# Normalised linear attention feeding a gated-convolution FFN on one core: the first head pair's three loads as fp32 on two hardware queues, three casts on two engines, and a new order

## The chip, the cores and the metric

The kernel runs on one core of one Trainium2 chip. A core has five engines with an instruction stream each: TensorE (matmul, written PE in the profile, its weight loads PEld), VectorE (DVE), ScalarE (ACT), GpSimd (POOL) and SyncE (SP), and 16 DMA engines which all of them feed. The metric is the device time of one execution in microseconds (us); lower is better. The kernel before takes 180.41 us, the median of three runs (180.30 to 180.98).

## The reference

For each of 8 batches and 8 heads (576 rows, head size 64) a 64x64 product of k and v is formed over the rows and applied to q. The rows of the result are normalised by their root mean square over the head, scaled by `g_norm`, and the heads are put side by side as rows of 512. A feed-forward part follows: a product with `w_in` (512 to 1024) and a ReLU, a three-tap convolution along the rows, a sigmoid of it as a gate, and a product with `w_out` (1024 to 512).

```python
kv = np.einsum('bhsd,bhse->bhde', k, v)
out = np.einsum('bhsd,bhde->bhse', q, kv)
rms = np.sqrt(np.mean(out * out, axis=-1, keepdims=True) + 1e-06)
x = (out / rms * g_norm).transpose(0, 2, 1, 3).reshape(B, S, H * D)
h = np.maximum(x @ w_in, 0.0)
hp = pad(h, 1)                                  # one zero row on either side
conv_out = sum(conv_w[k] * hp[:, k:k + S, :] for k in range(3))
gate = 1.0 / (1.0 + np.exp(-conv_out))
return (h * gate) @ w_out
```

Inputs and output are fp32; the kernel computes its products in bf16.

## The kernel before

The program is one list of tokens, `ORDER`, run from front to back. Each token is the name of a small operation with its arguments, such as `hm.0.3` for batch 0 and column block 3. Behind `@` stand the slots (PSUM banks, or places in a ring of SBUF buffers) that it takes, and behind `:` a choice of engine. At the end of the kernel a chain of dependences holds every engine to the order in which its instructions were emitted. So an engine never passes an instruction that waits, and the order decides who waits for whom. What `:1` means depends on the operation. For `kvc`, `kvn`, `ky`, `oc`, `re` and `ea` a plain token runs on ScalarE and `:1` on VectorE; for `qc0` and `qc` it is the other way round (helper `copy`, L337).

The work on batch 0 goes by head pairs t = 0 to 3, two heads in one 128-partition tile:

- `qt0.0.t` transposes q on TensorE (L378, 12 matmuls) and `qc0.0.t` copies it out of PSUM (L339 on ScalarE).
- `kv.0.t.1` forms the product of k and v (L356, 12 matmuls). `kvc.0.t.1.0` and `kvc.0.t.1.1` copy its two 64x64 blocks into the block-diagonal `kvbd`.
- `ot.0.t` applies it to q (L428 and L429, 64 and 512 columns). `sq` squares the result on ScalarE, `on` sums the squares over a head by a matmul with `ones`, `nl` takes the reciprocal root on ScalarE, and `mu0` multiplies on VectorE into the tile xT. For the last pair `sqh`, `onh`, `nlh` and `muh` do the same in halves.

Batch 1 takes two pairs at a time (`qt`, `qc`, `kv.1.t.2`), later batches four (`kv.b.0.4`, 48 matmuls). From batch 2 on the norm goes another way: `ss` gathers the sums of squares, `ln` takes the root, `sl` splits it into two bf16 parts, `sp` spreads it over the heads by matmuls (L601), and `mu` multiplies on VectorE.

The feed-forward part works by batch b and block f of 128 columns. `hm.b.f` is the product with `w_in` (L619, 8 matmuls), `re.b.f` the ReLU (L625 on ScalarE, L627 on VectorE). For a convolution group c of one or two batches, `ta`, `aa` and `ab` form the three taps on VectorE, `sg` the sigmoid on ScalarE (L680) and `mg` the gated product on VectorE (L686). `om.p.m.f0` is the product with `w_out` for 128 output rows (L696). `om` takes all eight blocks at once for p = 1 and 2; for p = 0 and 3 it takes four, so `om.3.m.0` needs the first four blocks and `om.3.m.4` the rest. `ea` copies it out and `st` stores it from SyncE. `oh`, `eh` and `sh` do the very last row block in two halves of 256 columns.

`unread.n` issues n matmuls on a constant tile, `fill`, into a bank that nobody reads (L425). They keep TensorE occupied where the order has nothing else for it.

The loads: `pre` (L215 to L239) issues those of batch 0. The first pair's k and v come as fp32 from SyncE's queue into a staging tile `stg`, and `ca` (L326) casts them to bf16 on VectorE. All other loads of q, k and v go out from GpSimd's queue, which casts to bf16 on the way: the first pair's q, then q, k and v of pairs 1 to 3. Between them GpSimd finishes the identity matrix (L236). `Lq`, `Lk` and `Lv` load the other batches, `Li` a quarter of `w_in` and `Lo` a half of `w_out`, all from GpSimd's queue. Two small rows, `g_norm` and the convolution weights, go out from ScalarE's queue (L221, L224) ahead of ScalarE's first table load (L211). `ct` transposes them on TensorE (L251), `pg` copies them out and `pc` prepares the weights. `pi`, `ps` and `pn` make small constants on VectorE.

Of the kernel before, what the change touches and what calls it, by code (L numbers as in the profile page):

```python
# [51 lines left out]
FP32 = mybir.dt.float32  # L52
# [11 lines left out]


ORDER = """
pre@0,0,0 pi unread.10@0 qt0.0.0@0 qc0.0.0:1@0 ps pn ca.k.0 ca.v.0 kv.0.0.1@1 kvc.0.0.1.0:1@0 kvc.0.0.1.1 Lq.1.0@1
ct@2 qt0.0.1@3 pg ot.0.0@0 pc unread.3@4 kv.0.1.1@2 Lk.1.0@1 qc0.0.1:1 kvc.0.1.1.0:1 Lv.1.0@1 sq.0.0@0 kvc.0.1.1.1:1
on.0.0@4 ot.0.1@2 qt0.0.2@6 nl.0.0@0 sq.0.1@1 unread.4@7 kv.0.2.1@7 on.0.1@4 qc0.0.2:1@1 al.x0@0 mu0.0.0 kvc.0.2.1.0
kvc.0.2.1.1:1 qt0.0.3@6 nl.0.1@1 ot.0.2@0 Li.0 unread.3@7 kv.0.3.1@7,4 mu0.0.1 sq.0.2@2 qc0.0.3:1 al.h0@0  # L70
kvc.0.3.1.0 on.0.2@2 kvc.0.3.1.1:1 ot.0.3@6 nl.0.2@2 sqh.0.3.0@3 Li.3 mu0.0.2 unread.3@5 onh.0.3.0@2 sqh.0.3.1
nlh.0.3.0@3 onh.0.3.1 Lq.1.2 nlh.0.3.1 qt.1.0@0 qc.1.0:1@2 Lv.1.2 unread.7@5 kv.1.0.2@0 muh.0.3.0 muh.0.3.1
kvc.1.0.2.0@1 kvc.1.0.2.1 unread.2@5 ot.1.1@0 sq.1.1@4 hm.0.0@6 on.1.1@2 hm.0.1@4 re.0.0 nl.1.1@4 ta.0.0@0 mu0.1.1
ot.1.0@6 hm.0.6@2 hm.0.7@0 Lk.1.2 re.0.1 sq.1.0@5 re.0.6 ta.0.1 aa.0.0 ta.0.6@1 on.1.0@2 qt.1.1@4 re.0.7 kv.1.2.2@0
nl.1.0@5 ab.0.0 qc.1.1@3 kvc.1.2.2.0 Li.1 kvc.1.2.2.1 ta.0.7 mu0.1.0 Lv.2.0@0 unread.3@1 ot.1.2@0 Li.2 Lk.2.0@0
ot.1.3@4 sq.1.2@6 unread.2@2 on.1.2@6 Lq.2.0@0 Lk.3.0@1 aa.0.3 sq.1.3@7 on.1.3@2 ab.0.3 nl.1.2@6 hm.0.3@6 nl.1.3@7
mu0.1.2 sg.0.0 hm.0.2@0 sg.0.1 re.0.2 mu0.1.3 hm.1.2@4 hm.0.5@2 sg.0.7 sg.0.6 re.0.3:1 Lv.3.0@1 pl mg.0.0 hm.1.3@6
hm.1.0@0 ta.0.2@0 al.x1@1 re.0.5 re.1.2 ta.0.3 re.1.0 mg.0.3 kv.2.0.4@2 aa.0.1 re.1.3 al.h1@1 ab.0.1 hm.1.1@4
ta.1.2@1 ta.1.3 hm.0.4@6 hm.1.7@0 aa.1.1 kvc.2.0.4.0@0 sg.0.2 sg.0.3 kvc.2.0.4.1 re.1.1 re.0.4 re.1.7 Lq.3.0@1
qt.2.0@2 qt.2.1@4 mg.0.1 hm.1.5@6 ab.1.1 ta.0.4@0 qc.2.0@4 Lo.0 sg.1.2 sg.1.3 ot.2.0@2 ta.0.5 hm.1.4@0 re.1.5  # L80
sq.2.0@0 qc.2.1@0 oc.2.0@0 mg.1.1 ot.2.2@4 ot.2.1@6 re.1.4:1 sq.2.2@1 kv.3.0.4@2 aa.0.2 oc.2.2@1 ot.2.3@0
kvc.3.0.4.0:1@1 sq.2.1@2 ab.0.2 ta.1.0@1 oc.2.1 sq.2.3@3 hm.1.6@4 ss.2@3 qt.3.1@6 re.1.6:1 sg.0.5 qt.3.0@4 oc.2.3
kvc.3.0.4.1:1 sg.0.4 qc.3.1@1 qc.3.0@2 ta.1.1 ln.8@0 unread.1@0 ot.3.3@6 unread.1@0 ot.3.0@4 Lo.1 ot.3.2@0 sq.3.0@4
mg.0.2 oc.3.0@2 Lq.4.0@0 aa.1.0 om.0.0.0@2 ta.1.4@0 sl.8@0 ta.1.5 ab.1.0 aa.1.2 sq.3.2@5 om.0.1.0@3 oc.3.2@3
om.0.2.0@4 sq.3.3@6 ot.3.1@0 om.0.0.4 oc.3.3 om.0.2.4 sq.3.1@7 oc.3.1 sp.2.0@6,0 ea.0.0@0 ss.3@5 ea.0.2@1 om.0.3.0@2
mu.2.0.0 ln.1@0 mu.2.0.1 sp.2.1@4,6 Lv.4.0@0 om.0.3.4 Lk.4.0@0 mu.2.1.0 qtp.4.0@0 sg.1.0 mu.2.1.1 sl.1@0 hm.2.6@4
qc.4.0:1@3 hm.2.2@6 re.2.6 ea.0.3@2 ab.1.2 re.2.2 sp.3.0@4,0 sg.1.4 sg.1.1 om.0.1.4 mu.3.0.1 mu.3.0.0 kv.4.0.4@2
sg.1.5 kvn.4.0.4 sp.3.1@0,6 ky.4.0.4.0 ea.0.1@3 hm.2.5@4 ky.4.0.4.1 re.2.5 mu.3.1.1 mu.3.1.0 hm.2.4@6 Lq.5.0@1
Lk.5.0@1 Lv.5.0@1 re.2.4 hm.3.4@0 mg.1.0 mg.1.2 oq.4.0@4 oq.4.1@2 re.3.4 hm.3.5@6 Lv.6.0@0 sq.4.0@0 ta.1.6@1
hm.3.7@0 oc.4.0@0 hm.3.3@4 re.3.5 sq.4.1@1 oc.4.1 re.3.7 Lk.6.0@0 ta.1.7 ta.2.4@0 qtp.4.1@6 aa.1.3 hm.2.3@2 ta.2.5  # L90
ab.1.3 om.0.7.0@0 re.3.3 qc.4.1@4 sg.1.7 sg.1.6 oq.4.2@6 oq.4.3@4 aa.2.2 mg.1.3 ab.2.2 re.2.3 kv.5.0.4@1 kvn.5.0.4:1
sq.4.2@2 oc.4.2@1 sq.4.3@3 hm.3.6@2 oc.4.3 re.3.6 sg.2.5 ky.5.0.4.0:1 qtp.5.1@6 al.x2@0 Lk.7.0@1 Lv.7.0@1 om.0.7.4
qc.5.1@0 ta.2.6@1 sg.2.4 qtp.5.0@2 ky.5.0.4.1:1 qc.5.0@1 hm.2.7@6 hm.3.2@4 re.2.7 oq.5.2@2 ea.0.7@4 oq.5.3@6
sq.5.2@4 re.3.2 Lq.6.0@0 oc.5.2@3 Lq.7.0@1 mg.2.2 om.0.6.0@1 om.0.4.0@0 ta.2.7 oq.5.0@4 oq.5.1@2 sq.5.3@5 oc.5.3
ta.2.2@0 om.0.4.4 sq.5.0@6 ss.4@6 sq.5.1@7 kv.6.0.4@7 ta.2.3 aa.2.3 ss.5 oc.5.0@2 hm.3.1@4 om.0.6.4 oc.5.1 aa.2.1
ln.2@0 ab.2.3 hm.3.0@2 re.3.1 kvn.6.0.4 ea.0.4@5 re.3.0 ea.0.6@6 sl.2@0 hm.2.1@4 ab.2.1 hm.2.0@6 sp.4.0@0,2 re.2.1
om.0.5.0@4 mu.4.0.0 mu.4.0.1 re.2.0 sp.5.1@6,0 mu.5.1.1 kv.7.0.4@5 om.0.5.4 st.0.1 st.0.0 dq.6.0@2 sp.5.0@0,2 st.0.7
kvn.7.0.4:1 kx.7.0.4.0 kx.6.0.4.0 sg.2.7 sg.2.3 kx.6.0.4.1 sg.2.2 sg.2.6 mu.5.1.0 mu.5.0.0 om.0.8.0@5 mu.5.0.1
sp.4.1@6,0 mu.4.1.0 mu.4.1.1 om.0.8.4 al.h2@0 dq.6.1@3 ea.0.8@7 st.0.3 hm.5.2@2 re.5.2 ea.0.5@3 dq.7.0@4 hm.4.2@6
st.0.2 mg.2.1 hm.5.0@0 mg.2.3 oq.6.0@4 re.4.2 ta.2.0@0 oq.6.1@2 re.5.0 sq.6.0@0 hm.5.7@6 oc.6.0@2 sq.6.1@1 dq.7.1@0  # L100
hm.5.3@0 hm.4.3@4 re.5.7 oc.6.1 oq.6.2@6 re.5.3 sq.6.2@2 re.4.3 oc.6.2@3 hm.4.5@2 ta.2.1 st.0.8 aa.2.0 hm.4.1@0
hm.5.5@4 hm.5.1@6 ta.3.2@1 ab.2.0 ta.3.3 re.4.5 sg.2.1 re.4.1 hm.4.0@2 sg.2.0 st.0.5 kx.7.0.4.1 re.5.1 re.5.5 re.4.0
aa.3.1 ab.3.1 hm.5.4@0 mg.2.0 hm.4.6@6 hm.4.4@4 re.5.4 om.1.5.0@0 ta.3.0@0 oq.7.0@2 re.4.6 sg.3.3 oq.6.3@6 sg.3.2
sq.7.0@3 ea.1.5@0 ta.3.1 sq.6.3@4 re.4.4 om.1.4.0@1 oc.6.3 oc.7.0@0 ea.1.4@4 al.x3@1 om.1.7.0@0 oq.7.2@2 oq.7.1@6
oq.7.3@4 aa.3.0 ea.1.7@2 ss.6@1 sq.7.1@5 sq.7.2@6 mg.3.1 om.1.6.0@0 sq.7.3@7 ab.3.0 oc.7.1 ss.7 ln.3@0 oc.7.2@1
om.1.3.0@6 ea.1.6@1 om.1.1.0@7 ta.3.4@1 ta.3.5 aa.3.2 oc.7.3 ab.3.2 sl.3@0 sp.7.0@4,0 mu.7.0.0 om.1.0.0@2 mu.7.0.1
sp.6.0@0,4 om.1.2.0@3 ea.1.3@7 sg.3.0 sg.3.1 ea.1.0@3 mu.6.0.0 mu.6.0.1 hm.5.6@4 mg.3.0 st.1.7 st.1.4 st.0.6 st.0.4
ea.1.2@2 sp.6.1@2,0 om.1.8.0@6 mu.6.1.1 sg.3.5 re.5.6 ea.1.1@4 mu.6.1.0 ea.1.8@6 ta.3.6@0 sp.7.1@2,4 hm.4.7@0
al.h3@1 re.4.7 mu.7.1.1 mu.7.1.0 hm.6.1@6 sg.3.4 hm.7.0@0 hm.6.0@2 hm.7.1@4 ta.3.7 re.6.1 hm.7.6@6 aa.3.3 mg.3.2
re.7.0 re.6.0 ab.3.3 re.7.1 re.7.6 hm.7.5@4 hm.6.2@6 hm.7.2@2 hm.7.3@0 sg.3.6 sg.3.7 re.6.2 re.7.5 hm.7.7@6 re.7.3  # L110
re.7.2 ta.4.0@1 re.7.7 ta.4.1 hm.6.3@4 hm.6.5@2 re.6.3 hm.6.4@4 hm.7.4@6 aa.4.0 mg.3.3 st.1.3 ab.4.0 ta.4.2@0 sg.4.0
sg.4.1 ta.4.3 re.6.4 aa.4.1 re.7.4 re.6.5 mg.4.0 ab.4.1 hm.6.6@0 hm.6.7@4 re.6.6 re.6.7 om.2.4.0@2 sg.4.3 om.2.2.0@3
om.2.1.0@4 om.2.7.0@5 om.2.6.0@0 om.2.3.0@1 sg.4.2 ta.4.4@1 ta.4.5 aa.4.2 ea.2.4@5 st.1.8 st.1.6 st.1.0 om.2.8.0@2
st.1.5 st.1.1 mg.4.1 ab.4.2 ea.2.2@7 ta.4.6@0 ta.4.7 aa.4.3 ea.2.1@6 sg.4.4 ea.2.7@1 sg.4.5 st.2.1 ab.4.3 ea.2.6@3
ea.2.3@0 mg.4.2 sg.4.7 sg.4.6 om.2.5.0@3 om.2.0.0@1 mg.4.3 om.3.1.0@0 ea.2.8@4 ea.2.5@6 st.2.2 st.2.8 om.3.3.0@3
oh.3.8.0@4 om.3.3.4 om.3.1.4 om.3.2.0@2 om.3.5.0@6 om.3.2.4 st.1.2 st.2.3 ea.2.0@7 eh.3.8.0@4 om.3.5.4 st.2.0
ea.3.3@2 st.2.4 om.3.0.0@3 ea.3.1@0 om.3.6.0@7 om.3.0.4 ea.3.2@7 ea.3.5@5 st.3.3 om.3.6.4 om.3.4.0@6 st.2.7
om.3.7.0@2 ea.3.0@2 om.3.4.4 st.3.2 om.3.7.4 ea.3.6@1 ea.3.4@7 st.3.5 st.3.1 st.2.5 st.3.0 st.2.6 st.3.6 sh.3.8.0
ea.3.7@5 st.3.4 st.3.7 oh.3.8.1 eh.3.8.1 sh.3.8.1
"""  # L120


# [1 line left out]
def kernel(  # L124
# [11 lines left out]
    nc = tc.nc  # L136
    B, H, S, D = q.shape
# [3 lines left out]
    R = 6  # L141
# [32 lines left out]
    def heads(x, b, h0, n):  # L174
        return src[x][b, h0:h0 + n].rearrange("h (p r) d -> p h (r d)", r=R)
# [39 lines left out]
    def pre():  # L215
        for x in "qkv":
            qkv[x, 0] = ring(x, [PS, H, R * D], BF16, name=x + "_sb")
        T["stg"] = work.tile([PS, 2, 2, R * D], FP32, name="stg", tag="h0", bufs=1)
        for i, x in enumerate("kv"):
            nc.sync.dma_start(out=T["stg"][:, i], in_=heads(x, 0, 0, 2))  # L220
        nc.scalar.dma_start(  # L221
            out=cw_rows[NC:].rearrange("p (i d) -> p i d", i=2),
            in_=g_norm.unsqueeze(0).unsqueeze(0).to_broadcast([1, 2, D]))
# [7 lines left out]
        for i in range(2):  # L231
            nc.vector.memset(ones[i * D:(i + 1) * D, i * D:(i + 1) * D], 1.0)
        nc.vector.memset(kvbd[1], 0.0)
        for n, (x, t) in enumerate([(x, t) for t in range(NT) for x in "qkv" if t or x == "q"]):
            if n == 2:
                nc.gpsimd.affine_select(  # L236
                    out=ident, in_=ident, compare_op=AL.not_equal, fill=1.0,
                    base=0, pattern=[[-1, P]], channel_multiplier=1)
            nc.gpsimd.dma_start(out=qkv[x, 0][:, 2 * t:2 * t + 2, :], in_=heads(x, 0, 2 * t, 2))  # L239
# [83 lines left out]

    @op
    def ca(x, t):
        nc.vector.tensor_copy(qkv[x, 0][:, 2 * t:2 * t + 2, :], T["stg"][:, "kv".index(x)])  # L326

    def last():
        return nc.cur_bb.bb.instructions[-1]
# [7 lines left out]
    def copy(to, fr, on_act):  # L337
        if on_act:
            nc.scalar.activation(to, fr, AX.Copy)  # L339
        else:  # L340
            nc.vector.tensor_copy(to, fr)
# [439 lines left out]
```

## Time and profile before

| | us |
|---|---|
| median of three runs | 180.41 |
| the profiled execution | 180.37 |
| its span, first to last instruction | 178.6 |
| idle TensorE from 20 to 40 us / from 40 to 60 us | 1.08 / 0.48 |
| first real matmul (L378) | 5.85 |
| first matmul of the feed-forward part (L619) | 19.61 |
| last matmul ends | 174.46 |

The page's second part shows the span in 40 equal slices of some 4.5 us; a digit is the busy share in tenths.

```profile
PE   6999997999999999999999999999999999999990
DVE  5544199799999899999999999968999999930000
ACT  2479679999999999999999999999789986853341
POOL 7985528005320210600000000000000000000000
DMA  5999999999999999999939700420340003046574
```

TensorE is occupied nearly everywhere, with the caution that a busy matmul row also holds fills. VectorE and ScalarE are lightly used in the first five slices and full from the sixth on. The DMA engines are busy from the second slice to about 90 us. Idle time of an engine that nobody waits for costs nothing, so the chain of waits and the timeline have to say which engine sets the pace in a given stretch.

### The profile page before, as it was taken

Reading aid. Unit: us, or ns where it says so; the run is one execution under the profiler, and the core shown is the slowest. Engines: PE = TensorE matmul, PEld = TensorE weight load, DVE = VectorE, ACT = ScalarE, POOL = GpSimd, SP = SyncE. Lnnn points to the kernel's source line nnn. Section 1 sums busy time; section 2 is a strip of 40 time slices with the busy share of each in tenths; the row PEclk is TensorE's granted clock in tenths of the full one; section 3 lists DMA queues with packets and bytes.
Section 4 is the critical chain, followed back from the end, with each engine's and each line's share of the span. In section 5 each row is a group of like instructions: output and inputs, shape, how many; then the busy total and the mean of one; then the engine's idle time right before and its main releaser. Section 6 shows DMA issues by size and latency. Waiting matters only on the chain.

```text
span 178.6 us, 4103 instructions
## 1 busy us (share of the span) xinstructions
PE 170.6 (96%) x1680; PEld 101.0 (57%) x1680; DVE 140.4 (79%) x238; ACT 149.2 (84%) x235; POOL 30.6 (17%) x54
## 2 busy tenths in 40 slices
PE   6999997999999999999999999999999999999990
PEld 2434664787545677737657774344678744445450
DVE  5544199799999899999999999968999999930000
ACT  2479679999999999999999999999789986853341
POOL 7985528005320210600000000000000000000000
PEclk9999999999999999999999999999999999999998
DMA  5999999999999999999939700420340003046574
GB/s 150 193 183 197 200 201 202 204 205 204 205 204 204 204 207 251 175 188 193 153 99 228 207 4 0 165 101 32 136 158 0 4 0 117 0 185 225 186 259 149
DMA packets 32619, 27.58 MB, mean 154 GB/s; under 512 B 6080, under 2 KB 28120, under 8 KB 32600
## 3 DMA queue, kind: packets, MB, share of 16 engines
q0 software_dynamic: 21760, 15.96, 59.0%
q1 hardware_dynamic: 10800, 11.34, 20.3%
q8 instruction: 13, 0.21, 0.5%
q14 instruction: 6, 0.05, 0.1%
q10 hardware_dynamic: 40, 0.01, 0.0%
HBM read 32.52 MB, written 9.44 MB: 235 GB/s over the span
## 4 chain that ended last, share of the span: by engine, by line
PE 76%; ACT 10%; DVE 4%; DMA 3%; POOL 3%; issue 2%; POOLq 0%; ACTq 0%
PE bank L696 35%; PE bank L619 27%; ACT taps L680 3%; DMA q_sb<-in_q_dram 3%; ACT h L625 3%; PE bank L356 3%; PE bank L425 2%; PE bank L601 2%; PE bank L462 2%; PE bank L429 1%; PE bank L386 1%; POOL q_sb L239 1%; PE bank L573 1%; ACT o L339 1%; PE bank L711 1%
## 5 line engine op out<-in xcount | busy, mean ns | idle before, releaser
L619 PE MATMUL bank<-xT,w_in_sb 128*128 128x288 bf16 x512 | 66.3, 286 | 0.6 <-ACT root L540 0.6
L696 PE MATMUL bank<-w_out_sb,h 128*128 128x512 bf16 x280 | 64.3, 380 | 0.0
L619 PEld LDWEIGHTS <-w_in_sb 128*128 128x128 bf16 x512 | 49.1, 98 | 15.2 <-issue 1.7
L696 PEld LDWEIGHTS <-h 128*128 128x128 bf16 x280 | 26.1, 98 | 30.5 <-issue 1.2
L680 ACT ACTIVATE taps<-taps,cwn 128x1152 bf16<-128x1152 bf16 (+1 forms) x40 | 41.4, 1087 | 2.1 <-DVE taps L674 2.0
L625 ACT ACTIVATE h<-bank 128x576 bf16<-128x576 f32 x61 | 38.5, 680 | 2.4 <-PE bank L619 1.7
L339 ACT ACTIVATE row<-bank 128x512 f32<-128x512 f32 (+1 forms) x37 | 21.6, 604 | 11.6 <-PE bank L696 8.5
L686 DVE TENSOR_TENSOR h<-h,taps 128x2304 bf16<-128x2304 bf16 (+1 forms) x20 | 22.1, 1114 | 2.5 <-ACT taps L680 2.4
L668 DVE TENSOR_TENSOR taps<-taps 128x2304 bf16<-128x2304 bf16 (+1 forms) x20 | 22.3, 1119 | 0.4
L674 DVE TENSOR_TENSOR taps<-taps,h 128x2304 bf16<-128x2304 bf16 (+1 forms) x20 | 22.3, 1113 | 0.2
L661 DVE TENSOR_SCALAR taps<-h,cwn 128x1152 bf16<-128x1152 bf16 (+1 forms) x40 | 18.6, 465 | 4.3 <-ACT h L625 4.3
L491 ACT ACTIVATE sq<-bank 128x576 bf16<-128x576 f32 x28 | 19.1, 712 | 1.0 <-PE bank L429 1.0
L608 DVE SCALAR_TENSOR_TENSOR xT<-o,cw,bank 128x576 bf16<-128x576 f32 x24 | 18.2, 810 | 1.6 <-PE bank L601 1.5
L662 DVE TENSOR_SCALAR taps<-h,cwn 128x1152 bf16<-128x1152 bf16 (+1 forms) x40 | 18.2, 455 | 0.0
L339 ACT ACTIVATE o<-bank 128x576 f32<-128x576 f32 x24 | 16.9, 725 | 0.0
L425 PE MATMUL bank<-fill 128*128 128x512 bf16 x39 | 12.4, 445 | 1.5 <-DVE fill L226 1.5
L211 ACT ACT_TABLE_LOAD x8 | 10.3, 1283 | 2.5 <-issue 2.4
L356 PEld LDWEIGHTS <-k_sb 96*64 96x64 bf16 x384 | 7.3, 113 | 3.3 <-issue 3.1
L299 POOL DMA_DIRECT2D q_sb<-in_q_dram x8 | 6.0, 752 | 16.1 <-PE bank L378 14.3
L356 PE MATMUL bank<-v_sb,k_sb 96*64 96x64 bf16 x384 | 8.3, 197 | 0.2
L299 POOL DMA_DIRECT2D k_sb<-in_k_dram x8 | 6.1, 765 | 13.7 <-PE bank L356 13.1
L299 POOL DMA_DIRECT2D v_sb<-in_v_dram x8 | 6.0, 751 | 12.6 <-PE bank L601 11.4
(83 smaller groups left out, 122.8 us busy)
## 6 DMA issues: line engine op xcount, KB each, us to landing
out_dram<-row SPq DMA_DIRECT2D x35, 256.0 KB, 2.5
v_sb<-in_v_dram POOLq DMA_DIRECT2D x6, 576.0 KB, 13.8
k_sb<-in_k_dram POOLq DMA_DIRECT2D x6, 576.0 KB, 14.1
q_sb<-in_q_dram POOLq DMA_DIRECT2D x6, 576.0 KB, 14.3
w_in_sb<-in_moe_w_in_dram POOLq DMA_DIRECT2D x4, 256.0 KB, 10.8
w_out_sb<-in_moe_w_out_dram POOLq DMA_DIRECT2D x2, 512.0 KB, 19.4
q_sb<-in_q_dram POOLq DMA_DIRECT2D x4, 144.0 KB, 4.4
q_sb<-in_q_dram POOLq DMA_DIRECT2D x2, 288.0 KB, 8.2
```

The lines of the kernel that those rows point to most:

```text
L339: nc.scalar.activation(to, fr, AX.Copy)
L356: nc.tensor.matmul(ps[i][i * D:(i + 1) * D, t - t0, :], k_sb[:, 2 * t + i, r * D:(r + 1) * D], v_sb[:, 2 * t + i, r * D:(r + 1) * D], star ...
L491: nc.scalar.activation(in_order(b, s), product(b, t), AX.Square)
L608: nc.vector.scalar_tensor_tensor(x_tile(b)[:, 2 * u:2 * u + 2, n], T["o32", b, u][:, :, n], g_sb, T["sp", b, e][u][:, :, :HS], op0=AL.mult ...
L619: nc.tensor.matmul(ps[:, e, :HS], w_in_sb[:, t, f * P:(f + 1) * P], x[:, t, e * HS:(e + 1) * HS], start=(t == 0), stop=(t == NT - 1))
L625: nc.scalar.activation(to, fr, AX.Relu)
L661: nc.vector.tensor_scalar_mul(tap[:, 0, f % 2, :n, 8:8 + S], h[:, f], cwn[:, 0, f:f + 1])
L668: nc.vector.tensor_add(tap[:, 1, :, :n, :S], tap[:, 0, :, :n, 7:7 + S], tap[:, 1, :, :n, 1:1 + S])
L674: nc.vector.tensor_add(y, y, h[:, 2 * j:2 * j + 2])
L680: nc.scalar.activation(y, y, AX.Sigmoid, scale=cwn[:, 1, f:f + 1])
L686: nc.vector.tensor_mul(h, h, T["tap", c, j][:, 1, :, :n, :S])
L696: nc.tensor.matmul(T["om", p, m], h[:, f, m * P:(m + 1) * P], w_out_sb[:, f, :], start=(f == 0), stop=(f == NF - 1))
```

## The change

It changes `pre`, `ca` and the whole of `ORDER`.

In `pre` the staging tile gets a third part. k goes out from SyncE, v from ScalarE's queue, then q from SyncE behind k. The two small rows follow v on ScalarE's queue. GpSimd no longer loads the first pair's q; its list begins with pair 1, and the identity is finished after the second of these loads, as before.

`ca` now takes any of the three and goes by its choice: `:1` is ScalarE, plain is VectorE. The new order has `ca.k.0:1`, `ca.v.0:1` and `ca.q.0`.

```diff
-        T["stg"] = work.tile([PS, 2, 2, R * D], FP32, name="stg", tag="h0", bufs=1)
-        for i, x in enumerate("kv"):
-            nc.sync.dma_start(out=T["stg"][:, i], in_=heads(x, 0, 0, 2))
+        T["stg"] = work.tile([PS, 3, 2, R * D], FP32, name="stg", tag="h0", bufs=1)
+        for i, x, queue in ((1, "k", nc.sync), (2, "v", nc.scalar), (0, "q", nc.sync)):
+            queue.dma_start(out=T["stg"][:, i], in_=heads(x, 0, 0, 2))
...
-        for n, (x, t) in enumerate([(x, t) for t in range(NT) for x in "qkv" if t or x == "q"]):
+        for n, (x, t) in enumerate([(x, t) for t in range(1, NT) for x in "qkv"]):
...
-        nc.vector.tensor_copy(qkv[x, 0][:, 2 * t:2 * t + 2, :], T["stg"][:, "kv".index(x)])
+        copy(qkv[x, 0][:, 2 * t:2 * t + 2, :], T["stg"][:, "qkv".index(x)], pick[0] == 1)
```

The order is new from front to back. Apart from `ca.q.0` and the fills it holds the same operations (694 tokens for 693). The fills are 40 instead of 39, in groups of 9, 1, 3, 1, 2, 3, 8, 3, 3, 2, 5 instead of 10, 3, 4, 3, 3, 7, 2, 3, 2, 1, 1. Its beginning, and the places that the prediction names (all groups of lines shortened):

```diff
-pre@0,0,0 pi unread.10@0 qt0.0.0@0 qc0.0.0:1@0 ps pn ca.k.0 ca.v.0 kv.0.0.1@1 kvc.0.0.1.0:1@0 kvc.0.0.1.1 Lq.1.0@1
-ct@2 qt0.0.1@3 pg ot.0.0@0 pc unread.3@4 kv.0.1.1@2 Lk.1.0@1 qc0.0.1:1 kvc.0.1.1.0:1 Lv.1.0@1 sq.0.0@0 kvc.0.1.1.1:1
...
-nlh.0.3.0@3 onh.0.3.1 Lq.1.2 nlh.0.3.1 qt.1.0@0 qc.1.0:1@2 Lv.1.2 unread.7@5 kv.1.0.2@0 muh.0.3.0 muh.0.3.1
...
-kvc.3.0.4.1:1 sg.0.4 qc.3.1@1 qc.3.0@2 ta.1.1 ln.8@0 unread.1@0 ot.3.3@6 unread.1@0 ot.3.0@4 Lo.1 ot.3.2@0 sq.3.0@4
...
-ea.2.3@0 mg.4.2 sg.4.7 sg.4.6 om.2.5.0@3 om.2.0.0@1 mg.4.3 om.3.1.0@0 ea.2.8@4 ea.2.5@6 st.2.2 st.2.8 om.3.3.0@3
-oh.3.8.0@4 om.3.3.4 om.3.1.4 om.3.2.0@2 om.3.5.0@6 om.3.2.4 st.1.2 st.2.3 ea.2.0@7 eh.3.8.0@4 om.3.5.4 st.2.0
+pre@0,0,0 al.x1@0 ca.k.0:1 pn ps ca.q.0 pi ca.v.0:1 unread.9@0 kv.0.0.1@0 kvc.0.0.1.0:1@0 qt0.0.0@1 Lq.1.0@1
+kvc.0.0.1.1:1 qc0.0.0:1@0 ct@2 pg pc qt0.0.1@3 ot.0.0@0 qc0.0.1:1 kv.0.1.1@2 al.x0@1 al.h1@0 Lv.1.0@1 Lk.1.0@1
+al.h0@1 sq.0.0@0 kvc.0.1.1.0:1 kvc.0.1.1.1:1 unread.1@4 on.0.0@4 qt0.0.2@3 nl.0.0@0 ot.0.1@6 sq.0.1@1 qc0.0.2:1@1
...
+unread.8@2 kv.1.0.2@6 Li.2 qc.1.0:1@2 kvc.1.0.2.0@1 muh.0.3.0 muh.0.3.1 kvc.1.0.2.1 unread.3@2 ot.1.1@6 hm.0.0@0
...
+ss.2@3 kvc.3.0.4.0:1@1 kvc.3.0.4.1:1 sg.0.4 mg.0.2 oc.2.1 unread.5@6 ot.3.2@0 ot.3.0@6 ln.8@0 re.1.5:1 sq.3.2@4
...
+ea.2.7@6 ea.2.3@1 om.2.2.0@5 mg.4.2 sg.4.7 sg.4.6 ea.2.6@0 om.3.0.0@0 om.3.5.0@4 ea.2.2@5 om.3.1.0@5 mg.4.3 om.3.5.4
+oh.3.8.0@2 om.3.1.4 om.3.0.4 om.3.6.0@1 om.3.7.0@6 st.2.7 st.2.1 st.1.1 om.3.4.0@7 st.2.8 ea.3.5@6 st.3.5 om.3.7.4
```

In the old order `kv.0.0` comes after `qt0.0.0`, in the new one before it. All eight `kvc` copies of batch 0 run on VectorE in the new order; in the old one ScalarE had one of the two of pairs 0, 2 and 3.

## The prediction

> **What bounds the kernel now.** I read the page first, then the chain of waits in order of time, the table by stages, the timeline of the first 20 us and the DMA view in slices of a microsecond.
>
> ```profile
> span 178.6 us, 4103 instructions
> PE 170.6 (96%) x1680; PEld 101.0 (57%) x1680; DVE 140.4 (79%) x238; ACT 149.2 (84%) x235; POOL 30.6 (17%) x54
> ...
> PE bank L696 35%; PE bank L619 27%; ACT taps L680 3%; DMA q_sb<-in_q_dram 3%; ACT h L625 3%; PE bank L356 3%; PE bank L425 2%; PE bank L601 2%; PE bank L462 2%; PE bank L429 1%; PE bank L386 1%; POOL q_sb L239 1%; PE bank L573 1%; ACT o L339 1%; PE bank L711 1%
> ```
>
> TensorE is busy 96% of the span, 12.4 us of it with matmuls on `fill` (L425), whose result nobody reads. The chain of waits (start, length, what) says where it is not TensorE:
>
> ```profile
> 6.39 5.57 DMA q_sb<-in_q_dram
> 12.01 0.45 PE bank L378 x12
> ...
> 18.20 0.52 PE bank L356 x24
> ...
> 47.00 0.77 DVE qT L341
> ...
> 49.13 2.59 PE bank L696 x12
> ```
>
> To 12.0 us it is loads, to 20 TensorE with fills, to about 48 ScalarE and VectorE by turns, and from there to 174.46 TensorE without a gap. The table by stages (length, then busy us of each engine) says the same:
>
> ```profile
> 5.85:20.00 14.15, 13.31 (x190) 6.92 (x190) 5.69 (x17) 10.22 (x21) 10.80 (x16) 1.00 1.32 192
> 20.00:40.00 20.00, 18.92 (x266) 13.79 (x263) 17.30 (x35) 18.21 (x31) 5.80 (x16) 1.00 1.33 203
> 40.00:60.00 20.00, 19.52 (x234) 11.06 (x228) 19.73 (x41) 19.94 (x34) 4.76 (x6) 1.00 1.30 204
> 60.00:80.00 20.00, 20.00 (x270) 13.33 (x269) 19.47 (x35) 19.91 (x35) 4.59 (x6) 1.00 1.26 206
> ```
>
> The columns are PE, PEld, DVE, ACT, POOL, clock, DMA share and GB/s. TensorE's work after 48.5 us is fixed, so a gain must come out of the first 48.5 us, while a loss can come anywhere. The head that the change edits:
>
> ```profile
> 4.48 0.55 DVE L326 CAST k_sb<-stg 96x768 bf16<-96x768 f32 x1
> 5.05 0.56 DVE L326 CAST v_sb<-stg 96x768 bf16<-96x768 f32 x1
> 5.85 0.66 PE L378 MATMUL bank<-ident,q_sb 96*64 96x96 bf16 x12
> 6.34 0.36 PE L356 MATMUL bank<-v_sb,k_sb 96*64 96x64 bf16 x12
> 7.50 0.20 PE L428 MATMUL bank<-qT,kvbd 128*128 128x64 bf16 x1 [0.26 <-ACT kvbd L339]
> ```
>
> The first transposes begin at 5.85 as q lands from POOL's queue; the first product `ot.0.0` is at 7.50.
>
> **The change, part by part.** *Landings.* SP issued k at 0.75 and v at 1.21; they landed 3.2 and 3.8 us later, at 3.95 and 5.0. Of hardware packets, 181 ran in the slice 2 to 3 us and 196 in 3 to 4, and a load has 192 (96 partitions by 2 heads), so a load costs the DMA engines 1.02 us. Now k and v start together at 0.75 on two queues, and q takes v's old place. The packets of k and v still end near 4.0, so v lands at up to 5.0, and k, if its packets alternate with v's, at 3.95 to 5.0. q's follow until 5.0 at best; v's semaphore came some 0.9 us behind the last of its packets, so q lands at 5.9, or 6.5 if software packets take turns with it. I take 6.1.
>
> A rule of the Trainium skill speaks against the split (DMA: Bandwidth & Descriptors, "Issuing engines are not separate DMA queues"): transfers issued by ScalarE, SyncE or GpSimd share the same 16 DMA engines and interleave, and a second issuer saves issue time only. By it v gains the 0.46 us between the two issues and k pays for it. No run here shows two such queues full at once, and by the rule the sum would be the one below.
>
> *Casts.* The trace has no ScalarE copy of 96x768. Its 128x576 copies take 0.65 and its 128x1152 copies 1.13, so 0.83 ns an element and 0.17 us; 768 give 0.81 against VectorE's 0.55. The table load (2.37 to 3.65) moves behind v's issue, about 0.4 us, to 4.07. So both casts end between 5.7 (k there at 3.95) and 6.6 (k there at 5.0), and `kv.0.0`, at 6.34 before, follows at 5.7 to 6.6. q's cast on VectorE runs 6.1 to 6.65; behind it on VectorE wait `pi`, 0.25 us, and both `kvc` copies; behind the casts on ScalarE waits `qc0.0.0`. Transposes 0.45, copy 0.65 and 0.1 for handing on bring `ot.0.0` to 7.85, 0.35 later than before (0.15 to 0.75).
>
> *Does that pass on?* Hardly. `kv.0.1`, `kv.0.2` and `kv.0.3` ran at 8.50, 11.13 and 13.47, 2.3 to 2.6 us apart; three software loads of 0.147 MB at the 0.192 MB/us of the DMA view take 2.3. The stream sets this pace, and fills the rest: 10 before `kv.0.3` in the old order, 7 in the new, 0.65 us of slack at 0.217 each. Without that cover the 0.35 would be paid in full.
>
> *The software stream.* POOL issues one load less, which is 0.77 us of stream; the hardware queues carry 192 packets more, 1.02 us. The slices show whether they add up:
>
> ```profile
> q1 hardware_dynamic: 196, 0.28, 106.1%
> q0 software_dynamic: 7, 0.01, 3.8%
> ```
>
> That is 3 to 4 us: software packets begin only at 3.9. From 5 to 7, alone, they run at 267 a microsecond; in 4 to 5, beside 53 hardware packets, 231. So 53 displaced 36, and 192 would displace 130, or 0.49 us: the stream then ends 0.28 early. If they add up, 0.25 late; if nothing is displaced, 0.77 early. I take 0.0, midway between the first two, since 31 of the 53 were short rows. The small rows themselves come some 0.4 us later and are wanted only by `ct`, at 6.63 before. At the end of this stream stands `kv.1.0` (18.13; POOL saw a v_sb load land at 18.11), now behind 8 fills instead of 7, covered by the fills saved earlier; uncovered they cost 0.22.
>
> *New order to the last fill.* Fills after `kv.1.0` go from 9 to 13, 0.87 us of TensorE. I summed start-to-start spacings (0.98 for an hm, 0.245 for an ot or on, 0.53 for a ScalarE pass over 576, 0.67 for a VectorE pass over 1152) over the tokens between `hm.0.0` and the last fill: TensorE without fills 24.1 before and 23.8 after, ScalarE 23.7 and 23.8, VectorE 25.1 and 25.1. The bound is the same, so the extra fills should sit where TensorE would wait for VectorE. From both sides: +0.7 if all lengthen the path; -0.7 if the last `kvc` on VectorE, which the product behind the fills waits for, comes after 24.4 us of its work instead of 25.1. I take +0.1.
>
> *From 48.5 on.* What TensorE still has to do is 126.1 before and 126.4 after, since the last fill stands one product earlier (that 0.3 is in the +0.7). VectorE finishes the last gate product `mg.4.3` at 158.57; the first matmul that needs it starts at 160.45, 1.9 us of slack. In the new order `om.3.5.4` needs it first; the smallest slack by the sums, from a spread product of the last batches to that point, is 3.2 instead of 3.6, so 1.5 should be left. For waits that no sum shows, 0 to 1.2 as in the rival below; I take +0.2. The last half-row `oh`, `eh`, `sh` ends both orders: 0.
>
> **Sum.** Span 178.6 + 0.0 + 0.1 + 0.2 = 178.9. The profiled execution took 180.37, 1.77 around its span; the runs have a median of 180.41, so no correction. Forecast **180.7 us**, no change that can be told (0.5%, 0.9 us, is about what can be).
>
> **Rivals.** *The stream gains the whole load.* q's packets displace nothing, `kv.1.0` and `hm.0.0` come 0.77 earlier, and half of the 0.7 before the last fill comes too: 180.4 - 0.77 - 0.35 = 179.3. For it: the software queue has no packet before 3.9 while the hardware queues carry two loads by then, and one cold fill less (0.43) is laid down. Against it: from 4 us on the DMA engines are busy in nearly every slice, and a load that is read as fp32 either way now lands at twice the bytes.
>
> *VectorE becomes the bound.* Slower. Place: the stretch from 48.5 to `om.3.5.4`, where VectorE is busy 19.5 to 19.7 of 20 us. By the sums, the slack from the spread products of batches 2 and 3 to the last gate product falls from 8.1-8.6 to 6.1-6.9 us, of batches 4 and 5 from 6.9-7.5 to 5.0-5.5. The sums flatter: where they say 3.6 the trace had 1.9. It decides once VectorE idles 1.5 us more than before; if the new order gives it another stretch like 20 to 40 us, 2.7 idle, TensorE waits 1.2: 181.9. Against it: 3 us should still be left in the middle.
>
> *q's packets take turns with the software stream from 3.9 on.* q lands at 6.5, `ot.0.0` at 8.25, and the stream is 0.25 late: 180.7 + 0.25 + 0.1 = 181.1. The Trainium skill has this rule too (DMA: Bandwidth & Descriptors, "Queues, rings and completion order": an engine goes round its queues, a packet at a time). The slice 4 to 5 agrees, both kinds ran in it (22 and 231).
>
> That the change does not start sooner at all is part of the forecast: q comes no earlier than by the software queue.
>
> **How the numbers follow.** Forecast 0.30, turns 0.14 (0.11 of it within 0.5%), whole load 0.25, VectorE 0.31. Faster 0.25; same 0.30 + 0.11 = 0.41; slower 0.31 + 0.03 = 0.34. The forecast's own range is 179.7 to 181.4 (the stream's -0.28 and the order's -0.7; +0.25 and +0.6). The range given, 179.2 to 182.4, takes in both other cases, and beyond 181.9 the VectorE case with half a microsecond more.
>
> **What would show it.** Right: the casts on ScalarE near 0.8 us, first transposes after 6.3, `ot.0.0` near 7.9, the 24-matmul L356 group of batch 1 within 0.3 of 18.1, its first L619 near 19.6, the last L425 done near 48.3, no idle TensorE behind it. Wrong: transposes of pair 0 before 5.8; that L356 group at 17.5 or earlier; TensorE idle over 0.5 us after 50 us, most of all ahead of L696 near 160; VectorE's last L686 later than 160.

## The result

| | before | changed |
|---|---|---|
| median of four runs, us | 180.38 | 182.11 |
| lowest and highest | 180.30 / 180.98 | 181.83 / 182.17 |
| ratio | | 1.0082, 95% interval 1.0060 to 1.0104 |
| profiled execution / its span | 180.37 / 178.6 | 182.07 / 180.3 |

The changed kernel is 0.8% slower. The time lies inside the range of the prediction and outside the forecast of no change; the reason is neither the forecast's nor that of any of its rivals.

The page of the changed kernel, its span, the busy time of its engines, and two of its DMA queues:

```profile
span 180.3 us, 4112 instructions
...
PE 172.7 (96%) x1681; PEld 101.9 (57%) x1681; DVE 141.8 (79%) x242; ACT 149.8 (83%) x232; POOL 29.6 (16%) x53
...
q0 software_dynamic: 21552, 15.81, 57.9%
...
q10 hardware_dynamic: 248, 0.31, 0.6%
```

The software queue (q0) has 208 packets fewer than before and ScalarE's queue (q10) 208 more, 192 of them a load: the loads moved as the diff says. TensorE is as full as before, but with 2.1 us more of what counts as busy, for the same work and one fill more.

The head in the timeline of the changed kernel (start, length, engine, line, output<-inputs, and in brackets idle time before it and what ended that):

```profile
1.47 4.02 PE L425 MATMUL bank<-fill 128*128 128x512 bf16 x9 [1.47 <-DVE fill L226]
...
5.35 0.84 ACT L339 ACTIVATE k_sb<-stg 96x768 bf16<-96x768 f32 x1 [1.27 <-DMA stg<-in_k_dram]
...
6.10 0.83 ACT L339 ACTIVATE v_sb<-stg 96x768 bf16<-96x768 f32 x1
...
6.80 0.56 DVE L341 CAST q_sb<-stg 96x768 bf16<-96x768 f32 x1 [2.26 <-DMA stg<-in_q_dram]
6.98 0.53 PE L356 MATMUL bank<-v_sb,k_sb 96*64 96x64 bf16 x12 [1.49 <-ACT v_sb L339]
...
8.89 0.23 PE L428 MATMUL bank<-qT,kvbd 128*128 128x64 bf16 x1
...
12.04 1.49 PE L425 MATMUL bank<-fill 128*128 128x512 bf16 x3
...
13.45 0.38 PE L356 MATMUL bank<-v_sb,k_sb 96*64 96x64 bf16 x12
...
20.43 0.57 PE L356 MATMUL bank<-v_sb,k_sb 96*64 96x64 bf16 x24
```

The same stretch of the kernel before:

```profile
1.47 4.45 PE L425 MATMUL bank<-fill 128*128 128x512 bf16 x10 [1.47 <-DVE fill L226]
...
6.80 0.45 PE L378 MATMUL bank<-ident,q_sb 96*64 96x96 bf16 x12
...
12.64 0.81 PE L425 MATMUL bank<-fill 128*128 128x512 bf16 x3
...
18.13 0.57 PE L356 MATMUL bank<-v_sb,k_sb 96*64 96x64 bf16 x24
```

Two things are to be seen. Everything of pair 0 is late: the first product is at 8.89 where it was at 7.50. And TensorE runs at half its pace until about 13.4 us. Twelve matmuls of L356 take 0.53 at 6.98 and 0.38 at 13.45; three fills take 1.49 at 12.04, and 0.81 at 12.64 in the kernel before. The kernel before had that slow pace too, its first ten fills standing 0.43 us apart, but left it at about 6: the twelve transposes at 5.85 still take 0.66, those at 6.80 take 0.45, as they do later. The changed kernel's nine fills end at 5.49, TensorE then stands still for 1.49 us, and the fast pace comes some 7 us later than before.

From there on nothing more is lost. Batch 1's first product of k and v (the group of 24 matmuls of L356) starts at 20.43 instead of 18.13, 2.30 later; the last matmul ends at 176.76 instead of 174.45, 2.31 later. The stage after the last fill, in the table by stages (stage, length, then busy us of PE, PEld, DVE, ACT and POOL, clock, DMA share, GB/s):

```profile
50.50:176.80 126.30, 126.08 (x1079) 73.40 (x1076) 106.11 (x152) 110.01 (x168) 5.38 (x7) 1.00 0.63 136
```

TensorE stands idle for 0.22 us of 126.3. The new order costs nothing after the head and gives back 0.6 at the end: from the last matmul to the end of the span it takes 3.5 us where the old one takes 4.1. Together 180.37 + 2.3 - 0.6 = 182.07, the profiled execution's time. The loss of 2.3 us is made before batch 1's L356 group.

### The profile page after: what moved, and what is told of

It reads as the page before. It is cut to its first block, busy times and chain, and to the rows that moved or that the text cites. A ratio compares the mean times of both kernels' runs of the same rounds, so it can differ in the third digit from the quotient of the medians.

```text
span 180.3 us, 4112 instructions
## 1 busy us (share of the span) xinstructions
PE 172.7 (96%) x1681; PEld 101.9 (57%) x1681; DVE 141.8 (79%) x242; ACT 149.8 (83%) x232; POOL 29.6 (16%) x53
## 4 chain that ended last, share of the span: by engine, by line
PE 76%; DVE 14%; ACT 4%; DMA 3%; issue 2%; ACTq 0%; DVEq 0%
PE bank L696 31%; PE bank L619 28%; PE bank L425 4%; PE bank L378 3%; PE bank L356 3%; DMA stg<-in_k_dram 3%; PE bank L429 2%; DVE taps L668 2%; DVE taps L674 2%; DVE taps L662 2%; DVE taps L661 2%; DVE h L686 2%; DVE xT L608 2%; PE bank L601 2%; PE bank L711 1%
## 5 line engine op out<-in xcount | busy, mean ns | idle before, releaser
L619 PE MATMUL bank<-xT,w_in_sb 128*128 128x288 bf16 x512 | 67.0, 286 | 0.3 <-ACT root L540 0.3
L339 ACT ACTIVATE row<-bank 128x512 f32<-128x512 f32 (+1 forms) x37 | 21.4, 594 | 13.4 <-PE bank L696 10.4
L491 ACT ACTIVATE sq<-bank 128x576 bf16<-128x576 f32 x28 | 18.3, 686 | 1.0 <-PE bank L429 1.0
L339 ACT ACTIVATE o<-bank 128x576 f32<-128x576 f32 x23 | 15.6, 705 | 0.0
L425 PE MATMUL bank<-fill 128*128 128x512 bf16 x40 | 13.3, 462 | 1.5 <-DVE fill L226 1.5
L356 PEld LDWEIGHTS <-k_sb 96*64 96x64 bf16 x384 | 7.4, 115 | 5.7 <-issue 3.9
L356 PE MATMUL bank<-v_sb,k_sb 96*64 96x64 bf16 x384 | 8.6, 200 | 1.5 <-ACT v_sb L339 1.5
L299 POOL DMA_DIRECT2D v_sb<-in_v_dram x8 | 6.0, 748 | 21.4 <-PE bank L601 13.7
L560 DVE SCALAR_TENSOR_TENSOR xT<-bank,cw,root 128x576 bf16<-128x576 f32 x7 | 5.6, 813 | 3.0 <-ACT root L540 3.0
## 6 DMA issues: line engine op xcount, KB each, us to landing
k_sb<-in_k_dram POOLq DMA_DIRECT2D x6, 576.0 KB, 13.7
```

The lines of the kernel that those rows point to most:

```text
L356: nc.tensor.matmul(ps[i][i * D:(i + 1) * D, t - t0, :], k_sb[:, 2 * t + i, r * D:(r + 1) * D], v_sb[:, 2 * t + i, r * D:(r + 1) * D], star ...
L619: nc.tensor.matmul(ps[:, e, :HS], w_in_sb[:, t, f * P:(f + 1) * P], x[:, t, e * HS:(e + 1) * HS], start=(t == 0), stop=(t == NT - 1))
```

## The experiments

Three theories were stated first: C, the pause keeps TensorE slow and that is the loss; L, pair 0's late operands are passed on; O, the new order is the slower one. Each ratio is to runs of the kernel before taken beside them; the last column is from one profiled execution.

| kernel | us, median | ratio to before, 95% interval | batch 1's L356 group at |
|---|---|---|---|
| new order, new loads, 15 fills | 180.08 | 0.9979 (0.9953 to 1.0004) | 18.32 |
| new order, old loads, 9 fills | 181.36 | 1.0035 (1.0001 to 1.0068) | 20.24 |
| old order, new loads, 10 fills | 182.20 | 1.0078 (1.0045 to 1.0111) | 19.81 |
| old order, old loads, 5 fills | 181.65 | 1.0074 (1.0049 to 1.0098) | 19.39 |
| new order, old loads, 13 fills | 179.91 | 0.9970 (0.9940 to 1.0001) | 18.11 |
| new order, three loads on one queue, 11 fills | 183.99 | 1.0173 (1.0136 to 1.0209) | 21.77 |
| new order, new loads, 15 fills, casts on VectorE | 180.02 | 0.9954 (0.9928 to 0.9979) | 18.67 |
| old order, new loads, 15 fills | 181.35 | 1.0036 (1.0012 to 1.0060) | 19.04 |
| new order, old loads, constants first, 10 fills | 181.38 | 1.0036 (1.0007 to 1.0065) | 20.06 |
| new order, old loads, 13 fills, 4 before batch 1 | 179.98 | 0.9972 (0.9955 to 0.9990) | 18.21 |
| new order, new loads, 15 fills, 4 before batch 1 | 179.80 | 0.9952 (0.9933 to 0.9971) | 17.96 |

**Fills over the pause.** One number of the changed kernel:

```diff
-unread.9@0 kv.0.0.1@0
+unread.15@0 kv.0.0.1@0
```

> Theory C (the pause before the first real matmul, 5.49 to 6.98 us, keeps TensorE at its slow starting pace to 13.4 us, and that is the loss): 15 fills instead of 9 reach over the pause, matmuls run at the fast pace from about 5.9 us on, the first product 128x512 takes 0.38 instead of 0.61, the 24-matmul L356 group of batch 1 starts at 18.5 to 19.0 instead of 20.43, and the time is 180.0 to 180.6. Theory L (pair 0's operands are 1.4 us late and that is passed on): the L356 group stays at 19.5 or later, time 181.5 to 182.1. Theory O (the new order is the slower one, wherever its loads come from): 182.1.

Measured 180.08. Its TensorE timeline:

```profile
1.47 5.67 PE L425 MATMUL bank<-fill 128*128 128x512 bf16 x15 [1.47 <-DVE fill L226]
...
7.07 0.38 PE L356 MATMUL bank<-v_sb,k_sb 96*64 96x64 bf16 x12
...
10.60 0.81 PE L425 MATMUL bank<-fill 128*128 128x512 bf16 x3
...
18.32 0.57 PE L356 MATMUL bank<-v_sb,k_sb 96*64 96x64 bf16 x24
```

The first real matmul starts no earlier than in the changed kernel (7.07 for 6.98), and still batch 1 comes 2.1 us earlier, a little earlier than C had it. Six matmuls that nobody reads are worth the whole loss. That is C, against L and O.

**The pause alone, in the kernel before.** `unread.10` becomes `unread.5`; operands, loads and order stay.

> The kernel before with 5 fills at the start instead of 10, nothing else. C: a pause from 3.7 to 5.85 us, slow matmuls for some 4 us and more behind it (a product 128x512 at 0.61), the L356 group of batch 1 at 19.5 to 20.5, time 181.3 to 182.5. L and O: operands and order are unchanged, 180.4.

```profile
1.47 2.31 PE L425 MATMUL bank<-fill 128*128 128x512 bf16 x5 [1.47 <-DVE fill L226]
6.32 0.69 PE L378 MATMUL bank<-ident,q_sb 96*64 96x96 bf16 x12 [2.54 <-DMA q_sb<-in_q_dram]
...
8.57 1.49 PE L425 MATMUL bank<-fill 128*128 128x512 bf16 x3
...
19.39 0.57 PE L356 MATMUL bank<-v_sb,k_sb 96*64 96x64 bf16 x24
```

Measured 181.65, as C has it, with the L356 group 0.1 us before its range; L and O had 180.4. In this profile q landed at 6.3 instead of 5.85, so about 0.5 us of the lateness is not the pause's.

**Order and loads taken apart.** First the new order with the loads and casts of before, then the old order with the new ones.

```diff
-        for i, x, queue in ((1, "k", nc.sync), (2, "v", nc.scalar), (0, "q", nc.sync)):
-            queue.dma_start(out=T["stg"][:, i], in_=heads(x, 0, 0, 2))
+        for i, x in enumerate("kv"):
+            nc.sync.dma_start(out=T["stg"][:, i], in_=heads(x, 0, 0, 2))
...
-        for n, (x, t) in enumerate([(x, t) for t in range(1, NT) for x in "qkv"]):
+        for n, (x, t) in enumerate([(x, t) for t in range(NT) for x in "qkv" if t or x == "q"]):
...
```

> The new order with the loads and casts of before (q by GpSimd's queue, k and v cast on VectorE). C and L both: no pause, since the casts end at 5.6 where the fills end at 5.5; first product near 7.4, time 179.7 to 180.4 (the tail behind the last matmul was 0.6 us shorter in the new order). O: 182.

Measured 181.36, with single runs from 179.80 to 182.03. The expectation was wrong about the pause: the new order puts `pn`, `ps` and `pi` between the two casts on VectorE, v's cast ran at 5.9, and TensorE stood still from 5.49 to 6.60. Its pace stayed slow to about 13.7. The profiled execution, at 182.03, is the slowest of the ten, so 20.24 in the table belongs to that end of the spread, not to the median.

In the old order only the beginning is new (line shortened):

```diff
-pre@0,0,0 pi unread.10@0 qt0.0.0@0 qc0.0.0:1@0 ps pn ca.k.0 ca.v.0 kv.0.0.1@1
+pre@0,0,0 pi ps pn ca.k.0:1 ca.v.0:1 ca.q.0 unread.10@0 qt0.0.0@0 qc0.0.0:1@0 kv.0.0.1@1
```

> The old order with the new loads and the three casts, fills as before (10, to 5.9 us). C: the pause is from 5.9 to about 7.4 us; if the fast pace was reached with the tenth fill and 1.5 us do not undo it, 180.6 to 181.3; if they do, 182 or more, with the first product 128x512 at 0.61. L: 181.5 to 182.0 at the fast pace. O: 180.4.

Measured 182.20, C's second case. Here the fast pace was reached before the pause, and lost again behind it:

```profile
1.47 4.23 PE L425 MATMUL bank<-fill 128*128 128x512 bf16 x10 [1.47 <-DVE fill L226]
6.84 0.45 PE L378 MATMUL bank<-ident,q_sb 96*64 96x96 bf16 x12 [1.14 <-DVE q_sb L341]
...
10.22 0.61 PE L429 MATMUL bank<-sq,ones 128*128 128x512 bf16 x1
...
13.39 0.38 PE L429 MATMUL bank<-sq,ones 128*128 128x512 bf16 x1
```

Transposes at 6.84 are fast, a product at 10.22 is slow, one at 13.39 fast again. So here a pause of 1.14 us was followed by a slow stretch, and it began only some 2 us after the pause had ended. Not every execution seems to pay: the ten took 181.40 to 183.42, and the fastest three, up to 181.68, are near the 181.35 that this version takes without a slow stretch (below).

**The new order at the fast pace.** The new order with the old loads and `unread.13`:

> The new order with the loads and casts of before and 13 fills instead of 9, so that they reach to the first real matmul (6.60 in the run with 9). C: no pause, the first product 128x512 at 0.38, the L356 group of batch 1 at 17.9 to 18.6, time 179.5 to 180.2, and no runs near 182. O: 181 or more.

Measured 179.91, the L356 group at 18.11; one run of twelve was at 181.96, against the expectation. Its mean granted clock is 0.991, that of the others 0.996 or more (the last section says what that tells). The new order is not the slower one: O falls. The median is 0.6 us lower than before, as much as its end is shorter, though the interval still reaches 1.

**The old order at the fast pace.** The old order with the new loads and `unread.15`:

> The old order with the new loads, the three casts and 15 fills, so without a pause. C: the fast pace throughout, the first product 128x512 at 0.38, 180.3 to 181.0; what is left above 180.4 is what the late operands cost the old order. L: 181.5 or more at the fast pace.

Measured 181.35, over what C had and under what L had. The pace is fast in spite of a pause of 0.74 us, yet:

```profile
7.21 0.45 PE L378 MATMUL bank<-ident,q_sb 96*64 96x96 bf16 x12 [0.74 <-DVE q_sb L341]
...
19.04 0.57 PE L356 MATMUL bank<-v_sb,k_sb 96*64 96x64 bf16 x24
```

The first product came 1.15 us later than before (8.65), batch 1's L356 group 0.91 later, and the time is 0.83 above that of the kernel before. So L is right in part for the old order: it passes most of the lateness on. The new order, at the fast pace, takes a first product that is 0.95 later (8.45) almost without loss (18.32 against 18.13). The old order has 10 fills between pair 0 and pair 3 and the new one 7, which fits; no run varied these fills alone.

**One queue for all three.** v goes to SyncE's queue between k and q; 11 fills.

> The changed kernel with v on SyncE's queue between k and q, so that all three are on one queue, and 11 fills. If the split over two queues is what holds k back, k lands near 4.0 us, v near 5.0 and q at 5.9 to 6.5, and ScalarE's first cast starts near 4.0 instead of 5.0 to 5.35; if the three fp32 loads as such do it, k lands at 4.6 or later again. C: no pause to speak of, first product 128x512 at 0.38, time 179.6 to 180.3.

The casts of the staging tile in the tile's own view (operation, count, lengths in ns, then start of first and last):

```profile
L339 ACT ACTIVATE k_sb<-stg x1: 842/842/842, 3.8 to 3.8; 96x768 bf16<-96x768 f32 x1
L339 ACT ACTIVATE v_sb<-stg x1: 842/842/842, 6.4 to 6.4; 96x768 bf16<-96x768 f32 x1
L341 DVE CAST q_sb<-stg x1: 555/555/555, 7.8 to 7.8; 96x768 bf16<-96x768 f32 x1
```

k lands at 3.8: it was the split that held it back. But v now lands at 6.4 and q at 7.8, both later than forecast. The software stream runs beside them from 4 us on, as it ran beside v's last packets before; that it is the reason is not shown. TensorE paused at 5.99 for 1.3 us and later for 0.78, was slow from 9.0 to about 15.7, and the time, 183.99, is the worst of all. The time was expected at 179.6 to 180.3, so the landings were mis-sized, and 11 fills did not reach to them.

**Casts.** All three on VectorE in the order k, v, q, 15 fills.

> The changed kernel with 15 fills and all three casts on VectorE, in the order k, v, q. Each cast 0.55 to 0.6 instead of 0.84, but the first real matmul stands behind the fills, at 7.1 as before, and q lands last in any case: 179.9 to 180.3, the same as with ScalarE's casts. Sharing the casts between two engines is then worth nothing here. 0.4 us or more either way would say that it matters.

Measured 180.02 against 180.08: sharing the casts between two engines is worth nothing that shows here, where the first real matmul stands behind 15 fills.

**Small constants first.** The new order, the old loads, `pi ps pn` ahead of the casts, 10 fills.

> The new order with the loads of before, the small constants (pi, ps, pn) ahead of the two casts on VectorE, and 10 fills. The casts then run at 4.5 and 5.05 as in the kernel before instead of 4.0 and 6.0, the first real matmul starts near 5.9 with no pause, first product 128x512 at 0.38 near 7.4. Theory P (once the pace is fast, the loads of batch 1 and the fills in front of them set the pace, so an earlier pair 0 is worth nothing): 179.7 to 180.2, as with 13 fills (179.91). If pair 0 still sets it: 179.2 to 179.5.

Measured 181.38, single runs from 180.06 to 182.32. In the profile v landed only at 6.6, TensorE paused for 1.55 us at 5.92, and the pace was slow from 10.0 to 13.0. So theory P was not tried by it; the run shows instead how much the landing of a load varies here.

**What stands behind the fills before batch 1.** In both versions without a pause `unread.8` becomes `unread.4`.

> The new order with the loads of before and 13 fills at the start, and 4 fills instead of 8 in front of batch 1's first product of k and v. If the load stream stands behind those fills, the L356 group of batch 1 starts at 17.7 or later, waiting for a load, where it was 18.11, and the time is 179.5 to 180.0. If the fills were what held it, it starts near 17.25 and the time falls to 179.0 to 179.5.

```profile
18.21 0.57 PE L358 MATMUL bank<-v_sb,k_sb 96*64 96x64 bf16 x24 [0.90 <-DMA k_sb<-in_k_dram]
```

> The changed kernel with 15 fills at the start and 4 instead of 8 in front of batch 1's first product of k and v. GpSimd saw batch 1's q land at 14.47 with the new loads and at 15.20 before, so the software stream looks 0.4 to 0.7 us earlier; if that is so and it can be used, the L356 group of batch 1 starts at 17.4 to 17.7 instead of 18.32 and the time is 179.2 to 179.8. If it is not, 18.0 or later and 179.8 to 180.2.

```profile
17.96 0.57 PE L356 MATMUL bank<-v_sb,k_sb 96*64 96x64 bf16 x24 [0.84 <-DMA k_sb<-in_k_dram]
```

(L358 is L356 there, that kernel being two lines longer.) Without the fills TensorE waits for k's load in both. So the load stream sets this point, and with the new loads it is 0.25 us earlier, in one profile each; that lies between the two cases of the second expectation. The second kernel has the lowest median of all, 179.80, below the kernel before (0.9952, 0.9933 to 0.9971) and the changed one; from the other versions without a slow stretch in the new order (179.91 to 180.08) it cannot be told.

## Why the prediction was right or wrong

- **The sum.** 180.7 was forecast and 182.11 measured: 1.4 off, inside the range, on the wrong side of 0.5%. That the range holds it is luck: its upper end was laid down for a VectorE that becomes the bound, and no term of the forecast or of a rival stands for what cost the 2.3 us. The forecast's own range, added up from its terms, is 179.6 to 181.5 and not 179.7 to 181.4; the time lies outside both.
- **The step that failed** is "Does that pass on? Hardly." It priced fills as slack in TensorE's work and missed that they hold its pace. One slow fill less and a first product of k and v at up to 6.6 both stood in the prediction, and ten fills had ended at 5.92, so a pause of up to 1.1 us could be read from it; what a pause does was not asked. The experiment with 15 fills prices it at 2.1 us of batch 1's 2.3.

  The Trainium skill has the gate (TensorE: Matmul & The Clock Gate, "Part 1: The HAM clock gate"): half pace at first, full pace after about 3.4 us of steady work, half again after an idle window of that length. The start agrees roughly: fifteen fills on end took 5.01, 5.30, 5.67 and 6.06 us in four profiles, which by the two spacings of 0.43 and 0.217 puts the change 3.2 to 5.3 us after the first fill (an estimate). The last part does not: pauses of 1.14, 1.30 and 1.55 us after the fast pace had been reached were followed by a slow stretch.
- **Landings** were mis-sized. k was put at 3.95 to 5.0 and landed at 5.33 in the changed kernel, at 4.8 to 5.0 in other runs with the same loads; v, put at up to 5.0, landed at about 5.7 (5.0 after its issue), hidden behind k's cast; q was put at 6.1 and landed at 6.80, elsewhere at 6.2 to 6.5. ScalarE's cast was right, 0.84 for 0.81. `ot.0.0` was put at 7.85 and came at 8.89, half a microsecond of that being slow transposes and copies behind them.
- **The cover** by fewer fills fits what was measured, once the pace is fast: batch 1 came 0.19 late with the new order and 0.91 with the old one.
- **The software stream** was taken at 0.0; the two profiles in which TensorE waits for it show 0.25 early, near the bound of 0.28 worked out from the slice 4 to 5 us.
- **The new order** was taken at +0.1 and +0.2 after batch 1 and measured at 0.0: from batch 1's L356 group to the end of the last matmul it is 156.3 us before and after. The end was taken at 0 and gave 0.6 back.
- **The rivals.** VectorE as the bound: it finished its last gate product at 160.30, past the 160 that was named as a sign, but the whole stage stood 2.3 us later, and TensorE waited for nothing. The direction that this rival stood for came true, its mechanism did not. The turns with the software stream: q's lateness came true, 0.3 beyond the rival's; the stream was not late. The whole load gained: no.

## What to carry to other kernels

Work that only keeps TensorE occupied belongs to the timing of the loads behind it. Whoever moves the first operands has to let it reach to the first real matmul, with a margin for how much a landing, and the moment at which the fast pace comes, vary from run to run. When a change moves a start, compare how long the same matmul takes before and after, not only when it begins; a busy share of 96% in both hides it. And a slack that one order has for a late start another may not have, so loads and order are best tried apart.

## What the runs showed of the hardware that was not expected

- **The pace of TensorE.** A product of 128x512 takes 0.61 at the slow pace and 0.38 at the fast one, fills stand 0.43 and 0.217 us apart. A pause of 0.74 us was harmless in one run. Pauses of 1.1 to 1.55 us were followed by slow stretches: to 13.4 in the changed kernel, 8.8 to 12.2 with the old order and new loads, 9.0 to 15.7 with one queue, 9.8 to 13.2 with the constants first. TensorE had shorter gaps behind these pauses too; whether the length of a pause, its place or the gaps behind it decide, no run separates.
- **The granted clock shows only some of it.** In the changed kernel's profile it reads 1.00 from the start, through all of the slow stretch. Where the fast pace had been reached and was lost again, it reads 0.50 for that time. The rows of two pages, the changed kernel and then the old order with the new loads, in 40 slices of some 4.5 us and in tenths (9 is 90% or more); the 6 stands for 9.0 to 13.5 us:

```profile
PEclk9999999999999999999999999999999999999999
...
PEclk9969999999999999999999999999999999999998
```

  So a slow start has to be read from the durations.
- **The kernel before can lose the pace too.** Of its 89 runs beside the experiments, seven have a mean granted clock of 0.986 or 0.987 over the span, the others 0.994 or more. These seven took 181.67 to 182.21 us, against a median of 180.5 for all. Four others took 181.85 to 182.05 with nothing to see in that number; no trace of them was kept.
- **Two hardware queues at once.** In the slice 2 to 3 us the changed kernel moved 103 packets on both queues; one queue alone had moved 181. With 15 fills it was 103 again.

```profile
q1 hardware_dynamic: 73, 0.11, 54.3%
q10 hardware_dynamic: 30, 0.05, 20.0%
```

  Their share of the DMA engines' time is lower too, 74% for 81%, so the engines were waiting in part; why, no run here tells. Two queues did not finish two loads sooner than one. k lost 0.9 to 1.4 us, and v, issued 0.46 us earlier, landed about 0.7 later in the changed kernel.
- **A load's landing is not a number.** v's load from SyncE's queue landed 3.8 us after its issue in the kernel before and 5.4 us after it in one run with the same loads.
